# Channel attention with a feed-forward: a fixed order for VectorE's first operations, 24 chunks multiplied early, another layout of the weights

## The chip, the cores and the metric

One Trainium2 chip, of which the program uses one core. The metric is the device time of one execution in microseconds (us), the median of three runs; lower is better.

## The reference

Four batches of q, k and v, each 6080 x 256. The columns of q and k are normalised over the 6080 rows, their 256 x 256 product is put through a softmax, v is multiplied by it, and the result goes through a feed-forward of width 2048 with a leaky ReLU.

```python
qn = q / (np.linalg.norm(q, axis=1, keepdims=True) + 1e-06)
kn = k / (np.linalg.norm(k, axis=1, keepdims=True) + 1e-06)
s = kn.transpose(0, 2, 1) @ qn / tau
a = softmax(s)            # over the last axis, with its maximum taken off
x = (v @ a).reshape(B * S, D)
h = x @ w_in
return np.maximum(0.01 * h, h) @ w_out
```

## The kernel before, in words

Each batch goes through two steps. **Scores:** q and k are read in 48 chunks of up to 128 rows, two chunks to a group and a load. A chunk's product adds to a 256 x 256 sum in PSUM (`Scores.product`), its squares to the column norms (ScalarE squares, VectorE adds). When all chunks are in, the norms, the softmax and its transpose follow (`norms_mm` to `turned_low`). **Feed-forward:** softmax and `w_in` are first multiplied into one matrix per batch (`w_product`, four blocks j, `win` being the split `w_in`), so that a tile of v needs two products only. The first is done in the seven-product scheme of Strassen and Winograd: `w_parts` makes seven weight blocks (A11, A22, A12, S1 to S4) from a block's copy `w_a`, `v_parts` seven operands from a tile of v.

Precision: a float32 value is split into a high part in float32r (a cast) and the rest (a subtraction), and a product is three matmuls in float32r (high-high, high-low, low-high: `PASSES`). A chunk that is multiplied without a split goes through plain float32 matmuls (line 171), one with a split through six float32r ones (line 176).

There are 24 tiles of v of 1024 (or 960) columns with 8 pairs p each, 192 windows in all. A window makes 21 matmuls of the first product (`block_product`, line 546), the activations (`leaky`), and 24 of the second one pair later (`ffn_out`, line 592, on `wo`, the split `w_out`). Side work is queued by window and taken out in slots (`put`, `slot`). The scores of batch b+1 run so beside the feed-forward of batch b.

The start is written out by hand. Batch 0's scores come first. Then the norms and softmax of batch 0, while `fill` multiplies and squares the first 2 x FILL chunks of batch 1 without a split; then `v_parts` of tile 0, `w_product` of block 0 and `w_parts`, then window 0. Blocks 1 to 3 of the weights follow in windows 0 to 6 (`w_early`), and the rest of `w_in` and `w_out`, which come as float64 bits, is converted there (`f64_split`, lines 317 to 333, on tile `f_raw`). Nothing but `tc.issue_after` orders VectorE's operations in the start; a scheduler places the rest. All loads and stores go through one queue, SyncE's.

Of the kernel before, what the change touches and what calls it, by code (L numbers as in the profile page):

```python
# [17 lines left out]
P = 128  # L18
TW = 512
G = 2  # L20
# [3 lines left out]
FILL = 5  # L24
# [7 lines left out]
def channel_attention_ffn(  # L32
# [50 lines left out]
    nc.vector.memset(ones, 1.0)  # L83
    zeros = const.tile([P, P], F32, name="zeros")
    nc.vector.memset(zeros, 0.0)
    exp_bias = const.tile([P, 1], F32, name="exp_bias")
    nc.vector.memset(exp_bias, -896.0 * 2.0**23)
# [16 lines left out]
    class Scores:  # L104


        def __init__(self, b, sizes):
            self.b, self.groups, self.of = b, [], {}
            for n in sizes:
                at = sum(len(x) for x in self.groups)  # L110
                self.of.update({at + x: (len(self.groups), x) for x in range(n)})
                self.groups.append(range(at, at + n))
            self.raw, self.split = {}, {}

        def begin(self, acc, s):
            self.acc, self.s = acc, s
# [45 lines left out]
        def product(self, j):  # L162
            first, last = j == 0, j == NCHUNK - 1
            sp = self.split.pop(j, None)
            raw = self.chunk(j)
            if first:
                nc.tensor.matmul(out=self.s, lhsT=zeros, rhs=raw, start=True, stop=False, skip_group_check=True)
            for h in range(CH):
                hs, s = slice(h * P, (h + 1) * P), self.s[:, h * C:(h + 1) * C]
                if sp is None:  # L170
                    mm = nc.tensor.matmul(  # L171
                        out=s, lhsT=raw[:, 1, hs], rhs=raw[:, 0, :], start=False, stop=last, skip_group_check=True
                    )
                    continue
                for n, (y, z) in enumerate(((0, 0), (0, 1), (1, 0))):
                    mm = nc.tensor.matmul(  # L176
                        out=s, lhsT=sp[:, 1, y, hs], rhs=sp[:, 0, z, :], start=False, stop=last and n == 2,
                        skip_group_check=True,
                    )
            return mm  # L180


        def sums(self):

            acc, other = self.acc
            nc.vector.tensor_tensor(out=acc, in0=acc, in1=other, op=ALU.add)
            nc.vector.tensor_tensor(out=acc[:, :, 0, :], in0=acc[:, :, 0, :], in1=acc[:, :, 1, :], op=ALU.add)
            self.acc = [acc[:, :, 0, :]]
# [190 lines left out]
    A11, A22, A12, S1, S2, S3, S4 = range(NS)  # L379
# [31 lines left out]
    def w_parts(b, j):  # L411
# [71 lines left out]
    wo = const.tile([P, 2, NF, C], F32R, name="w_out_split")  # L483
    FPB = TW // C

    def wo_block(i):
        fs = slice(i * FPB, (i + 1) * FPB)

        def split(raw):
            f64_split(raw, *(wo[:, x, fs, :].rearrange("p f d -> p (f d)") for x in range(2)))  # L490

        return w_out.rearrange("(f p) d -> p f d", p=P)[:, fs, :], split
# [45 lines left out]
    PASSES = ((0, 0), (0, 1), (1, 0))  # L538
# [39 lines left out]
    def ffn_out(i, p):  # L578
# [7 lines left out]
        for name, f, j in (("C11", f1, 0), ("C22", f2, 1), ("C21", f2, 0), ("C12", f1, 1)):  # L586
            sp = g_split.pop((i, p, name))
            early = name in ("C11", "C22")
            for h in range(CH):
                for k, (x, y) in enumerate(((0, 0), (1, 0), (0, 1))):  # L590
                    with in_order("pe"):
                        issued["pe"] = nc.tensor.matmul(  # L592
                            out=o_ps[i][j][h][:, 0:n],
                            lhsT=wo[:, x, f, h * P:(h + 1) * P],
                            rhs=sp[:, y, 0:n],
                            start=p == 0 and early and k == 0,
                            stop=p == NPAIR - 1 and not early and k == 2,
                        )
                    yield
# [47 lines left out]
    def chunk_work(sc, j):  # L647

        put("act", 0.6, lambda: sc.cast(j), [
            ("dve", 0.75, lambda: sc.low(j), [("pe_next", 1, lambda: sc.product(j))]),  # L650
        ])
        if j == 0:
            sc.begin([acc_tile()], bank("s"))
# [90 lines left out]
    for b in range(1, B):  # L744
        w0 = (b - 1) * WPB
        sc = scores[b]
        done = FILL * G if b == 1 else 0
        begin_at, span = (NPAIR, 25) if b == 1 else (2, 31)
        when = {j: w0 + begin_at + (j - done) * span // (NCHUNK - done) for j in range(done, NCHUNK)}
        for i in range(done // G, len(sc.groups)):  # L750
            at(max(w0, when[i * G] - 3), lambda sc=sc, i=i: sc.load(i, qk_raw()))
        for j in range(done, NCHUNK):
            at(when[j], chunk_work, sc, j)
# [9 lines left out]
    sc.begin(  # L763
        [work.tile([P, 2, G, C], F32, name="sq_acc0", tag="qk_split", bufs=3) for _ in range(2)], bank("o", 4)
    )
# [14 lines left out]
    tau_t = const.tile([P, 1], F32, name="tau_t")  # L780
    nc.sync.dma_start(out=tau_t, in_=tau.partition_broadcast(P))
    rtau = const.tile([P, 1], F32, name="rtau")
# [11 lines left out]
    sc.sums()  # L794
    sc.norms_mm()
    sc.norms_taken()
    sc.norms_begun()
    after["dve"] = sc.norms()
    with tc.issue_after(after["load"].ins):
        for i in range(min(2, FILL)):  # L800
            nxt.load(i, qk_raw())
    sc.rows_mm()
    sc.rows_taken()
    after["scaled"] = sc.scaled()
    sc.exps()
    after["normed"] = sc.normed()
    nxt.begin([acc_tile()], bank("s"))
    filled = []

    def fill(n):  # L810
        for i in range(len(filled), min(len(filled) + n, FILL)):
            for j in nxt.groups[i]:
                nxt.product(j)
                if j == 0:
                    nxt.square(j, nxt.acc[0])
                else:
                    sq = temp(name="sq").rearrange("p (x c) -> p x c", x=2)
                    nxt.square(j, sq)
                    nxt.add_square(sq)
            if i + 2 < FILL:  # L820
                nxt.load(i + 2, qk_raw())
            filled.append(i)

    with tc.issue_after(after["dve"].ins):
        fill(2)
    sc.turn("x")
    sc.turned_high()
    after["turned"] = sc.turned_low()
    with tc.issue_after(after["scaled"].ins):
        fill(1)  # L830
        for _, fn in v_parts(0):
            fn()
# [3 lines left out]
    for _, fn in w_parts(0, 0):  # L836
        fn()
    with tc.issue_after(after["turned"].ins):
        fill(FILL)

# [82 lines left out]
```

## Time and profile before

| | |
|---|---|
| median of three runs | 2238.57 us (2238.31 to 2239.28) |
| the profiled execution's own time | 2239.86 us |
| its span | 2238.1 us |
| TensorE (PE) busy | 2189.6 us (98%), 9940 matmuls |
| VectorE (DVE) busy | 1492.8 us (67%) |
| ScalarE (ACT) busy | 1488.8 us (67%) |
| mean granted clock of TensorE | 0.991 |

The chain that ended last is 91% PE. The share of busy time is a mean over stages: the first 210 us or so look different from the rest, and are shown by window below.

### The profile page before, as it was taken

How to read it: one execution, taken by the hardware profiler on the slowest of the kernel's cores; microseconds unless marked ns; L12 is line 12 of the kernel's file. 1: busy time of each engine (PE TensorE's matmuls, PEld its weight loads, DVE VectorE, ACT ScalarE, POOL GpSimd, SP SyncE). 2: the span in 40 equal slices, each digit the busy share in tenths (PEclk: the TensorE clock that was granted, in tenths of full speed). 3: DMA queues.
4: the chain of work that ended last, by engine and by line, in shares of the span. 5: the costliest groups of instructions: out<-in, count | busy, mean ns of one | idle time of the engine just before them, and what ended most of it. 6: DMA issues, size and time to landing. Idle time of an engine off the chain costs nothing.

```text
span 2238.1 us, 27253 instructions
## 1 busy us (share of the span) xinstructions
PE 2189.6 (98%) x9940; PEld 1815.0 (81%) x9940; DVE 1492.8 (67%) x2651; ACT 1488.8 (67%) x2563; POOL 2.8 (0%) x10
## 2 busy tenths in 40 slices
PE   9689999999999999999999999999999999999999
PEld 7467888888888888888887888888888888888887
DVE  7986667666766676666767667677577655555554
ACT  6556777766657777776656777777666666666665
POOL 0000000000000000000000000000000000000000
PEclk9789999999999999999999999999999999999999
DMA  9445343342753434433464344343354432333330
GB/s 347 144 149 191 119 158 138 130 148 84 244 198 111 158 132 137 160 113 139 147 220 164 116 147 156 120 158 129 110 197 149 159 122 85 134 120 104 114 118 35
DMA packets 98966, 324.74 MB, mean 145 GB/s; under 512 B 10256, under 2 KB 22032, under 8 KB 98832
## 3 DMA queue, kind: packets, MB, share of 16 engines
q1 hardware_dynamic: 98832, 323.00, 41.9%
q8 instruction: 78, 1.28, 0.2%
q14 instruction: 56, 0.46, 0.1%
HBM read 264.50 MB, written 58.46 MB: 144 GB/s over the span
## 4 chain that ended last, share of the span: by engine, by line
PE 91%; DVE 5%; ACT 2%; DMA 1%; issue 0%; SPq 0%; DVEq 0%
PE ps_o L592 44%; PE ps_x L546 22%; PE ps_z L546 11%; PE ps_y L546 5%; PE ps_s L176 4%; PE ps_o L171 2%; PE ps_s L395 1%; DVE h L567 1%; DVE g_split L560 1%; ACT h L557 1%; ACT g_split L558 1%; DMA w_dram<-w_rest 1%; DMA f_raw<-in_w_out_dram 0%; DVE w_split L434 0%; DVE v_split L511 0%; DVE f_x L328 0%
## 5 line engine op out<-in xcount | busy, mean ns | idle before, releaser
L592 PE MATMUL ps_o<-g_split,w_out_split 128*128 128x512 f32 (+1 forms) x4608 | 1175.9, 391 | 0.0
L592 PEld LDWEIGHTS ps_o<-g_split,w_out_split 128*128 128x128 f32 x4608 | 868.5, 188 | 180.1
L560 DVE TENSOR_TENSOR g_split<-h,g_split 128x512 fp32r<-128x512 f32 (+1 forms) x768 | 525.4, 684 | 396.1 <-ACT g_split L558 394.6
L546 PE MATMUL ps_x<-v_split,w_split 128*128 128x512 f32 (+1 forms) x2304 | 658.5, 394 | 27.3 <-DVE w_split L433 15.6
L557 ACT ACTIVATE h<-h 128x512 f32<-128x512 f32 (+1 forms) x576 | 362.0, 628 | 290.1 <-DVE h L567 290.1
L573 ACT COPY h<-ps_x 128x512 f32<-128x512 f32 (+1 forms) x576 | 334.3, 580 | 321.8 <-PE ps_x L546 320.4
L546 PEld LDWEIGHTS ps_x<-v_split,w_split 128*128 128x128 f32 x2304 | 423.6, 189 | 118.3 <-ACT h L573 12.0
L558 ACT CAST g_split<-h 128x512 fp32r<-128x512 f32 (+1 forms) x768 | 473.7, 617 | 24.0
L567 DVE TENSOR_TENSOR h<-ps_z,h 128x512 f32<-128x512 f32 (+1 forms) x384 | 262.0, 682 | 293.1 <-ACT h L573 286.5
L546 PE MATMUL ps_z<-v_split,w_split 128*128 128x512 f32 (+1 forms) x1152 | 324.5, 390 | 5.3 <-DVE h L567 5.3
L546 PEld LDWEIGHTS ps_z<-v_split,w_split 128*128 128x128 f32 x1152 | 216.5, 188 | 54.0 <-DVE h L567 7.2
L546 PE MATMUL ps_y<-v_split,w_split 128*128 128x512 f32 (+1 forms) x576 | 163.0, 392 | 0.6 <-ACT w_a L405 0.6
L567 DVE TENSOR_TENSOR h<-ps_y,h 128x512 f32<-128x512 f32 (+1 forms) x192 | 131.3, 684 | 1.9
L546 PEld LDWEIGHTS ps_y<-v_split,w_split 128*128 128x128 f32 x576 | 109.1, 190 | 23.4 <-ACT w_a L405 1.1
L176 PEld LDWEIGHTS ps_s<-qk_split 128*128 128x128 f32 x804 | 114.0, 188 | 12.1 <-issue 1.0
L557 ACT ACTIVATE h<-ps_x 128x512 f32<-128x512 f32 (+1 forms) x192 | 113.1, 589 | 9.6 <-PE ps_x L546 9.6
L176 PE MATMUL ps_s<-qk_split 128*128 128x256 f32 x804 | 117.9, 282 | 0.0
L154 ACT CAST qk_split<-qk_raw 128x512 fp32r<-128x512 f32 x134 | 82.9, 619 | 32.4 <-PE ps_s L176 24.6
L511 DVE TENSOR_TENSOR v_split<-v_raw,v_split 128x512 fp32r<-128x512 f32 (+1 forms) x144 | 98.7, 687 | 4.7
L149 DVE TENSOR_TENSOR sq_acc<-sq_acc,sq 128x512 f32<-128x512 f32 x141 | 96.2, 683 | 0.0
L158 DVE TENSOR_TENSOR qk_split<-qk_raw,qk_split 128x512 fp32r<-128x512 f32 x134 | 91.7, 684 | 2.4 <-ACT qk_split L154 2.4
L146 ACT ACTIVATE sq<-qk_raw 128x512 f32<-128x512 f32 x141 | 88.6, 632 | 1.7 <-DMA qk_raw<-in_k_dram 1.7
(101 smaller groups left out, 728.4 us busy)
## 6 DMA issues: line engine op xcount, KB each, us to landing
w_split<-w_dram SPq DMA_DIRECT2D x184, 896.0 KB, 4.7
qk_raw<-in_q_dram SPq DMA_DIRECT2D x92, 256.0 KB, 3.3
qk_raw<-in_k_dram SPq DMA_DIRECT2D x92, 256.0 KB, 3.7
v_raw<-in_vT_dram SPq DMA_DIRECT2D x40, 512.0 KB, 4.9
out_dram<-o_sb SPq DMA_DIRECT2D x80, 256.0 KB, 4.2
win<-win_dram SPq DMA_DIRECT2D x24, 512.0 KB, 4.2
w_dram<-w_rest SPq DMA_DIRECT2D x24, 512.0 KB, 3.1
w_dram<-w_first SPq DMA_DIRECT2D x24, 384.0 KB, 3.1
```

The source lines that it names most:

```text
L146: return nc.scalar.activation(out=out, in_=self.chunk(j), func=AF.Square)
L149: return nc.vector.tensor_tensor(out=self.acc[0], in0=self.acc[0], in1=sq, op=ALU.add)
L158: return nc.vector.tensor_tensor(out=sp[:, :, 1, :], in0=self.chunk(j), in1=f32(sp[:, :, 0, :]), op=ALU.subtract)
L176: mm = nc.tensor.matmul(out=s, lhsT=sp[:, 1, y, hs], rhs=sp[:, 0, z, :], start=False, stop=last and n == 2, skip_group_check=True,)
L511: last = nc.vector.tensor_tensor(out=sp[:, 1, 0:w], in0=src, in1=f32(sp[:, 0, 0:w]), op=ALU.subtract)
L546: mm = nc.tensor.matmul(out=ps[:, 0:n], lhsT=w[:, x, a, :], rhs=sp[:, y, 0:n], start=first and k == 0, stop=k == 2, skip_group_check=True,)
L557: nc.scalar.activation(out=out[:, 0:n], in_=h[:, 0:n], func=AF.Prelu, alpha=0.01)
L558: issued["act"] = nc.scalar.copy(out=sp[:, 0, 0:n], in_=out[:, 0:n])
L560: issued["dve"] = nc.vector.tensor_tensor(out=sp[:, 1, 0:n], in0=out[:, 0:n], in1=f32(sp[:, 0, 0:n]), op=ALU.subtract)
L567: issued["dve"] = nc.vector.tensor_tensor(out=h[:, 0:n], in0=ps[:, 0:n], in1=h[:, 0:n], op=ALU.add)
L573: issued["act"] = nc.scalar.copy(out=h[:, 0:n], in_=ps[:, 0:n])
L592: issued["pe"] = nc.tensor.matmul(out=o_ps[i][j][h][:, 0:n], lhsT=wo[:, x, f, h * P:(h + 1) * P], rhs=sp[:, y, 0:n], start=p == 0 and earl ...
```

## The change

Four edits. First, `ordered` gives VectorE one order in the start: the norms, the softmax, `v_parts`, `w_parts`, with the softmax first. Second, `FILL` goes from 5 to 12 groups: 24 chunks of batch 1 are multiplied in the start instead of 10, from their own buffers (`qk_fill`, in the ring of `g_split`); they are no longer squared there, but loaded again and squared in windows 8 to 18 (`chunk_work` with `multiply=False`). Third, in batch 0 the casts of `w_parts` and of tile 0's `v_parts` move from VectorE to ScalarE. Fourth, the blocks of `w_split` stand in another order, `PASSES` takes low weights before low operands, and the two halves of `wo` get 128 columns between them.

```diff
-FILL = 5
+FILL = 12
...
+    wo_hl = const.tile([P, 2 * NF * C + P], F32R, name="w_out_split")
+    wo = [wo_hl[:, x:x + NF * C].rearrange("p (f d) -> p f d", d=C) for x in (0, NF * C + P)]
...
-    A11, A22, A12, S1, S2, S3, S4 = range(NS)
+    S1, S2, S3, S4, A22, A12, A11 = range(NS)
...
-                nc.vector.tensor_copy(out=hi, in_=src)
+                (nc.vector.tensor_copy if b else nc.scalar.copy)(out=hi, in_=src)
...
-        nc.vector.tensor_copy(out=sp[:, 0, 0:w], in_=src)
+        (nc.vector.tensor_copy if i else nc.scalar.copy)(out=sp[:, 0, 0:w], in_=src)
...
-    PASSES = ((0, 0), (0, 1), (1, 0))
+    PASSES = ((0, 0), (1, 0), (0, 1))
...
-    def chunk_work(sc, j):
+    def chunk_work(sc, j, multiply=True):
+        if multiply:
+            put("act", 0.6, lambda: sc.cast(j), [
+                ("dve", 0.75, lambda: sc.low(j), [("pe_next", 1, lambda: sc.product(j))]),
+            ])
...
+        quick = 10 if done else 0
+        when = [w0 + begin_at + j * quick // max(done, 1) for j in range(done)]
+        when += [w0 + begin_at + quick + j * (span - quick) // (NCHUNK - done) for j in range(NCHUNK - done)]
...
+            with tc.issue_after(after["load"].ins):
+                nxt.load(i, work.tile([P, 2, G, C], F32, name="qk_fill", tag="g_split", bufs=GBUFS))
             for j in nxt.groups[i]:
                 nxt.product(j)
-                if j == 0:
-                    nxt.square(j, nxt.acc[0])
...
+    ordered(sc.norms_taken, sc.norms_begun, sc.norms)
+    sc.rows_mm()
+    parts = [fn for _, fn in v_parts(0)]
+    ordered(parts[0], sc.rows_taken, sc.scaled)
+    sc.exps()
+    ordered(parts[1], sc.normed)
+    sc.turn("x")
+    sc.turned_high()
+    ordered(parts[2], parts[3], sc.turned_low)
...
+    ordered(*parts[4:8])
+    ordered(*(fn for _, fn in w_parts(0, 0)))
+    ordered(*parts[8:])
+    fill(FILL)
```

On PE, from the end of batch 0's scores to window 0, this stands before (`ps_s` is batch 1's sum, line 194 the norms, 248 the scale's rows, 291 the transpose, 395 the product with `w_in`):

```order
L167 MATMUL ps_s<-qk_raw,zeros 128x512
L171 MATMUL ps_s<-qk_raw 128x256 x8
L194 MATMUL ps_y<-ones,sq_acc_124 128x1 x4
L171 MATMUL ps_s<-qk_raw 128x256 x8
L248 MATMUL ps_y<-diag,ones 128x128 x2
L171 MATMUL ps_s<-qk_raw 128x256 x4
L291 MATMUL ps_x<-ident,s_sb 128x128 x4
L395 MATMUL ps_y<-win_early,aT 128x512 x4
L395 MATMUL ps_z<-win_early,aT 128x512 x4
```

And this with the change, at the same place:

```order
L200 MATMUL ps_y<-ones,sq_acc_126 128x1 x4
L254 MATMUL ps_y<-diag,ones 128x128 x2
L171 MATMUL ps_s<-qk_fill,zeros 128x512
L180 MATMUL ps_s<-qk_fill 128x256 x12
L297 MATMUL ps_x<-ident,s_sb 128x128 x4
L180 MATMUL ps_s<-qk_fill 128x256 x11
L401 MATMUL ps_y<-win_early,aT 128x512 x6
L401 MATMUL ps_z<-win_early,aT 128x512 x6
L180 MATMUL ps_s<-qk_fill 128x256 x25
L551 MATMUL ps_x<-v_split,w_split 128x512 x3
```

The early chunks moved behind the rows of the scale, 12 of their 48 matmuls stand ahead of the transpose, 11 ahead of the product with `w_in`, 25 behind it and ahead of window 0.

On DVE, from the scale (`diag`) to just behind the softmax's maxima (`nm`), this stands before:

```order
L240 TENSOR_SCALAR diag<-ident,rn 128x128 x2
L149 TENSOR_TENSOR sq_acc<-sq_acc,sq 128x512
L255 COPY rq<-ps_y 128x256
L149 TENSOR_TENSOR sq_acc<-sq_acc,sq 128x512
L260 SCALAR_TENSOR_TENSOR s_sb<-ps_o,rk,rq 128x256 x2
L149 TENSOR_TENSOR sq_acc<-sq_acc,sq 128x512
L266 TENSOR_REDUCE nm<-s_sb 128x2
L510 CAST v_split<-v_raw 128x512 x2
```

And this with the change:

```order
L246 TENSOR_SCALAR diag<-ident,rn 128x128 x2
L516 TENSOR_TENSOR v_split<-v_raw,v_split 128x512
L261 COPY rq<-ps_y 128x256
L266 SCALAR_TENSOR_TENSOR s_sb<-ps_o,rk,rq 128x256 x2
L272 TENSOR_REDUCE nm<-s_sb 128x2
L516 TENSOR_TENSOR v_split<-v_raw,v_split 128x512
L285 TENSOR_SCALAR den<-den 128x2
```

The additions of squares left this stretch, and one subtraction for v stands where PE makes the scale's rows, another where ACT takes the exponentials.

On ACT, in window 1, behind the copy of block 1 of the weights (`w_a`; `f_raw`, `f_scale` and `w_out_split` belong to the conversion of `w_out`, `h` and `g_split` to the activations), this stands before:

```order
L405 COPY w_a<-ps_y 128x512
L321 ACTIVATE f_scale<-f_scale,exp_bias 128x512 x2
L557 ACTIVATE h<-h 128x512
L558 CAST g_split<-h 128x512
L332 CAST w_out_split<-f_x 128x512 x2
L323 ACTIVATE f_raw<-f_raw 128x512 x2
L573 COPY h<-ps_x 128x512
```

And this with the change:

```order
L411 COPY w_a<-ps_y 128x512
L439 CAST w_split<-w_a 128x128 x2
L327 ACTIVATE f_scale<-f_scale,exp_bias 128x512 x2
L439 CAST w_split<-w_a 128x256 x2
L562 ACTIVATE h<-h 128x512
L563 CAST g_split<-h 128x512
L439 CAST w_split<-w_s 128x256 x2
L338 CAST w_out_split<-f_x 128x512 x2
L439 CAST w_split<-w_s 128x256 x2
L329 ACTIVATE f_raw<-f_raw 128x512
L578 COPY h<-ps_x 128x512
```

Eight casts came to ACT, four of them on `w_s`, which DVE adds up; they stand ahead of the next copy of `h`.

## Rows read from the trace of the kernel before

**Rows 1.** Windows: us, busy PE, PEld, DVE, ACT, POOL (instructions), PE clock, DMA, GB/s.

```profile
60.00:85.00 25.00, 11.60 (x30) 7.39 (x28) 25.00 (x59) 10.48 (x20) 0.00 (x0) 0.64 0.27 90
85.00:140.00 55.00, 46.26 (x171) 34.43 (x170) 43.94 (x93) 34.80 (x60) 0.00 (x0) 0.88 0.40 150
140.00:210.00 70.00, 57.79 (x235) 44.89 (x234) 54.28 (x115) 42.48 (x74) 0.00 (x0) 0.95 0.50 178
210.00:600.00 390.00, 390.00 (x1827) 325.46 (x1826) 265.34 (x466) 271.34 (x472) 0.00 (x0) 1.00 0.43 146
```

**Rows 2.** PE's longest wait in total, from 85 to 215 us.

```profile
PE ps_x L546 <- DVE w_split L433: 12.1, 3, 5.2
```

**Rows 3.** Timeline of PE, 40 to 62 us: start, us, instruction (two rows a matmul).

```profile
48.70 1.02 PE L167 MATMUL ps_s<-qk_raw,zeros 128*128 128x512 f32 x2
49.55 3.62 PE L171 MATMUL ps_s<-qk_raw 128*128 128x256 f32 x16
53.16 1.05 PE L194 MATMUL ps_y<-ones,sq_acc 128*128 128x1 f32 x8
...
57.80 0.68 PE L248 MATMUL ps_y<-diag,ones 128*128 128x128 f32 x4
59.23 1.99 PE L171 MATMUL ps_s<-qk_raw 128*128 128x256 f32 x8 [0.74 <-DMA qk_raw<-in_k_dram]
```

**Rows 4.** Timeline around the softmax: an addition of squares on DVE, the transpose on PE.

```profile
57.77 0.68 DVE L149 TENSOR_TENSOR sq_acc<-sq_acc,sq 128x512 f32<-128x512 f32 x1
...
66.92 1.17 PE L291 MATMUL ps_x<-ident,s_sb 128*128 128x128 f32 x4 [5.70 <-DVE s_sb L282]
```

**Rows 5.** Timeline of ACT and PE in window 0.

```profile
77.65 1.19 PE L546 MATMUL ps_x<-v_split,w_split 128*128 128x512 f32 x2 [3.53 <-DVE w_split L433]
89.26 0.59 ACT L573 COPY h<-ps_x 128x512 f32<-128x512 f32 x1 [1.97 <-PE ps_x L546]
91.27 0.84 PE L546 MATMUL ps_x<-v_split,w_split 128*128 128x512 f32 x3
```

**Rows 6.** Windows of half a microsecond in which the clock changed its level.

```profile
63.50:64.00 0.50, 0.00 (x0) 0.00 (x0) 0.50 (x2) 0.50 (x2) 0.00 (x0) 0.60 0.00 0
118.00:118.50 0.50, 0.50 (x3) 0.35 (x3) 0.50 (x2) 0.00 (x0) 0.00 (x0) 0.78 0.79 301
```

**Rows 7.** The page's group of split chunks; timeline of PE around one.

```profile
L176 PE MATMUL ps_s<-qk_split 128*128 128x256 f32 x804 | 117.9, 282 | 0.0
...
294.23 0.88 PE L176 MATMUL ps_s<-qk_split 128*128 128x256 f32 x6
294.95 0.88 PE L546 MATMUL ps_x<-v_split,w_split 128*128 128x512 f32 x3
295.66 0.85 PE L546 MATMUL ps_z<-v_split,w_split 128*128 128x512 f32 x3
296.35 1.31 PE L592 MATMUL ps_o<-g_split,w_out_split 128*128 128x512 f32 x5
297.50 0.85 PE L546 MATMUL ps_x<-v_split,w_split 128*128 128x512 f32 x3
```

**Rows 8.** Timeline of DVE and PE before block 1 of the weights is used.

```profile
104.96 0.42 DVE L317 TENSOR_SCALAR f_scale<-f_raw 128x512 int32<-128x512 int32 x1
112.46 0.42 DVE L433 CAST w_split<-w_a 128x128 fp32r<-128x128 f32 x2
112.83 1.71 PE L546 MATMUL ps_x<-v_split,w_split 128*128 128x512 f32 x3 [5.22 <-DVE w_split L433]
114.33 1.48 PE L546 MATMUL ps_y<-v_split,w_split 128*128 128x512 f32 x3
```

**Rows 9.** Timeline of DVE and PE where block 2 of the weights is first used.

```profile
145.47 0.42 DVE L421 TENSOR_TENSOR w_s<-w_a,w_s 128x256 f32<-128x256 f32 x1
146.17 1.19 PE L546 MATMUL ps_x<-v_split,w_split 128*128 128x512 f32 x2 [5.16 <-DVE w_split L433]
148.88 1.48 PE L546 MATMUL ps_y<-v_split,w_split 128*128 128x512 f32 x3
```

More of the change, by code (lines that the diff above doesn't have):

```diff
@@ L167, in product @@
                 nc.tensor.matmul(out=self.s, lhsT=zeros, rhs=raw, start=True, stop=False, skip_group_check=True)
-            for h in range(CH):
-                hs, s = slice(h * P, (h + 1) * P), self.s[:, h * C:(h + 1) * C]
-                if sp is None:
-                    mm = nc.tensor.matmul(
[L172 to L177, printed above, removed]
+            passes = [None] if sp is None else [(0, 0), (0, 1), (1, 0)]
+            for n, of in enumerate(passes):
+                for h in range(CH):
+                    hs, s = slice(h * P, (h + 1) * P), self.s[:, h * C:(h + 1) * C]
+                    if of is None:
+                        lhsT, rhs = raw[:, 1, hs], raw[:, 0, :]
+                    else:
+                        lhsT, rhs = sp[:, 1, of[0], hs], sp[:, 0, of[1], :]
+                    mm = nc.tensor.matmul(
+                        out=s, lhsT=lhsT, rhs=rhs, start=False, stop=last and n == len(passes) - 1,
                         skip_group_check=True,
@@ L645, in acc_tile @@
         return work.tile([P, 2, C], F32, name="sq_acc", bufs=1)
[L647 to L651 removed]
+    def chunk_work(sc, j, multiply=True):
[3 more added lines that the diff above has]
+            ])
         if j == 0:
[L653 removed]
+            sc.acc = [acc_tile()]
             put("act", 0.6, lambda: sc.square(0, sc.acc[0]))
@@ L748, in channel_attention_ffn @@
         begin_at, span = (NPAIR, 25) if b == 1 else (2, 31)
-        when = {j: w0 + begin_at + (j - done) * span // (NCHUNK - done) for j in range(done, NCHUNK)}
-        for i in range(done // G, len(sc.groups)):
+        quick = 10 if done else 0
+        when = [w0 + begin_at + j * quick // max(done, 1) for j in range(done)]
+        when += [w0 + begin_at + quick + j * (span - quick) // (NCHUNK - done) for j in range(NCHUNK - done)]
+        if b > 1:
+            at(when[0], lambda sc=sc: setattr(sc, "s", bank("s")))
+        for i in range(len(sc.groups)):
             at(max(w0, when[i * G] - 3), lambda sc=sc, i=i: sc.load(i, qk_raw()))
-        for j in range(done, NCHUNK):
-            at(when[j], chunk_work, sc, j)
+        for j in range(NCHUNK):
+            at(when[j], chunk_work, sc, j, j >= done)
         e = w0 + begin_at + span + 1
@@ L762, in channel_attention_ffn @@
     sc, nxt = scores[0], scores[1]
-    sc.begin(
-        [work.tile([P, 2, G, C], F32, name="sq_acc0", tag="qk_split", bufs=3) for _ in range(2)], bank("o", 4)
-    )
+    sc.acc = [work.tile([P, 2, G, C], F32, name="sq_acc0", tag="qk_split", bufs=3) for _ in range(2)]
+    sc.s, nxt.s = bank("o", 4), bank("s")
     n0 = len(sc.groups)
@@ L793, in channel_attention_ffn @@
             conv.split()
[L794 to L807, printed above, removed]
     filled = []
@@ L811, in fill, with ordered @@
         for i in range(len(filled), min(len(filled) + n, FILL)):
+            with tc.issue_after(after["load"].ins):
+                nxt.load(i, work.tile([P, 2, G, C], F32, name="qk_fill", tag="g_split", bufs=GBUFS))
             for j in nxt.groups[i]:
                 nxt.product(j)
-                if j == 0:
-                    nxt.square(j, nxt.acc[0])
[L816 to L821, printed above, removed]
-            filled.append(i)
-    with tc.issue_after(after["dve"].ins):
-        fill(2)
+            filled.append(i)
+    def ordered(*fns):
+        for fn in fns:
+            with in_order("dve"):
+                issued["dve"] = fn()
+    sc.sums()
+    issued["dve"] = sc.last_sum
+    sc.norms_mm()
+    ordered(sc.norms_taken, sc.norms_begun, sc.norms)
[4 more added lines that the diff above has]
+    ordered(parts[1], sc.normed)
     sc.turn("x")
     sc.turned_high()
[L828 to L832, printed above, removed]
+    ordered(parts[2], parts[3], sc.turned_low)
     for h in range(CH):
```

25 lines of the change are left out of this document (10 added, 15 removed).

## The prediction

> **What bounds the kernel now.** I read the windows first. From 210 to 600 us PE is busy 390.00 of 390.00 us at clock 1.00, while DVE has 265 and ACT 271 [rows 1]: there the time is PE's work, and only fewer or shorter matmuls change it. From 60 to 85 us it is the other way round: DVE is busy 25.00 of 25.00 and PE 11.60. From 85 to 210 PE lacks 55 - 46.26 + 70 - 57.79 = 20.9 us, and its clock is down at times [rows 1]. So I read next what PE waited for there: 12.1 us in three waits for DVE's casts of the weights, line 433 [rows 2]. The change therefore acts on two accounts: PE's work in the long stage, which is worth its full length, and the start, where it matters when DVE's chain lets PE go.
>
> **The moved products.** The page counts 804 matmuls of split chunks, six a chunk, so 134 of 192 - 48 = 144 chunks; ten of batch 1 went early. With 24 early, 14 x 6 = 84 float32r matmuls leave the long stage. One chunk there takes from 294.23 to 294.95, 0.72 us [rows 7], and PE has no gap to give it back: **-10.1 us**. This term is the firmest: nothing moves into PE's place. What ACT and DVE do instead (24 squares and additions for early chunks, no casts or lows for them) is about what they did before, 0.6 to 0.7 us an operation, in 30% and more of free time [rows 1]. Batch 1's first 12 groups are read twice now, 36 group loads for 24: some 6 MB more, on DMA engines that are 43% busy [rows 1], issued three windows ahead; I cost them at nothing. Without that lead a late group would cost its own landing, a few us.
>
> **The fill.** Sixteen rows, four plain chunks, took 3.62 us at full clock, 0.90 a chunk, and the opening matmul with zeros 0.85 [rows 3]. So the early work grows to 24 x 0.90 + 0.85 = 22.5 us, all of it ahead of window 0 in PE's order. It costs what it sticks out behind DVE's chain, so I lay out PE's time anew:
> - Batch 0's product ends at about 48.7 and the norms' matmuls still start at 53.16, the scale's rows at 57.80 [rows 3], since the chain of sums and Newton steps ahead of them is the same.
> - SyncE's queue puts seven transfers of 0.5 MB ahead of the first early group that stood behind it (two loads of `w_out`, two of `w_in`, three stores of `win`). The fifth early group, the 39th such transfer, landed at 59.2, and PE waited 0.74 us for it [rows 3]: some 1.4 us each, as an estimate. The first early group is now the 38th, so it lands at about 57.8, and the next ones come faster than PE's 1.8 a group. So the fill starts at about 58.4, behind the rows, and loads do not hold it. One load of `w_out` stands ahead of batch 0's last three groups: 1.4 us at most, which DVE's queue of additions covers. Behind the last early group stand only stores of block 0 and the load of tile 1, due windows later.
> - PE is then idle from 48.7 to 53.2 and from 54.2 to 57.8. In the trace the clock fell at 63.7 [rows 6], 2.5 us after PE's last matmul ended (59.23 + 1.99 = 61.2 [rows 3]). So I take it that the fill begins at the lower level, half the rate (1.2 for 2.4 GHz). From 112.83, where PE worked without a break, the clock came back at 118.2, after 5.4 us [rows 6, 8]. Half of that is lost: 2.6 us.
> - The transpose waits for 12 of the 48 fill matmuls now: 58.4 + 0.85 + 6 x 0.90 + 2.6 = 67.2. It started at 66.92 before, waiting for the softmax [rows 4]. That one gets faster by four additions of 0.6 us ahead of its maxima and sums [rows 4] and ends around 63; so the new order on DVE alone frees nothing, the fill takes its place.
> - Transpose (0.7) and the product with `w_in` (12 x 0.23, the step in [rows 7]) are added: window 0 starts at 58.4 + 22.5 + 2.6 + 0.7 + 2.8 = **87.0**, where its first matmul stood at 77.65 [rows 5]. By then `w_parts` is done: its input is there at about 76.5, and DVE needs some 7 us behind that.
> - Before, window 0 was torn by waits and at half clock; its sixth product began at 91.27 [rows 5]. Now: two products 1.4, drain 0.2, then DVE 0.69, ACT three times 0.6, a product 0.7, six matmuls 1.4 and hops 0.2 = 6.4 us, so 93.4. The start is **+2.1 us** later.
>
> At this place a rule speaks for another sum. By the Trainium skill, Perfetto Trace Analysis, section Engine Utilization, a float32 high-low matmul has half the normal rate. The rows disagree: 0.45 us against 0.12 for 256 columns, 3.8 times. By the page's figure the fill would be about 11 us, DVE's chain would set window 0 at about 83, and the time would be 2223 to 2224.
>
> **The blocks of weights in windows 2 and 4.** The high casts go to ACT. For block 1, DVE is busy without a gap from 104.96 to the cast at 112.46, and PE's matmul follows at 112.83 [rows 8]; the same additions and conversions stand ahead of the first subtraction now, 0.2 us long instead of the cast's. So PE's second matmul, which needs that low part, comes at about 112.8: only the first one is won, and the second product starts at 113.6 instead of 114.33 [rows 8], -0.7. For block 2 one conversion step (0.6) moved behind the subtraction, and the low half no longer comes 2 us after the high one: second product at 146.5 instead of 148.88 [rows 9], -2.4. Block 3 I leave at nothing. Sum **-3.1 us**. Both ends: nothing, if ACT's copies of `h`, which queue behind casts that wait for DVE's `w_s`, lose what is won (8 casts a block, 3 us on ACT); -8, if the waits of 12.1 us [rows 2] shrink by two thirds.
>
> **The layout.** No row shows a matmul with other distances. Two differ in the trace: three matmuls on `w_split`, whose halves lie 3,584 bytes apart, take 295.66 to 296.35, 0.230 each; five on `wo`, halves 16,384 bytes apart, 296.35 to 297.50, 0.230 each [rows 7]. Equal to a nanosecond, so I take nothing. One nanosecond over 8,640 matmuls would be 8.6 us; I keep that as both ends.
>
> **The sum.** -10.1 + 2.1 - 3.1 = -11.1. The profiled execution took 2239.86 us, 1.3 above the median of the runs, so 2228.8 on its own terms and 2238.57 - 11.1 = **2227.5** on the median's.
>
> **Rivals.**
> - *The fill stays at half clock* (slower). If the clock does not come back until PE's float32 matmuls are through, 22.5 us become 45 and with the transpose and the product behind it some 48: 20 to 23 more, 2248 to 2250. It decides from 28 us of half rate on, where the gain is used up (11.1 + 2.6 = half of 28). For it: no row shows the clock rising under float32 matmuls. Against it: it stood at 1.00 under the same instructions until 61 us. 6%.
> - *The clock is not lost, or DVE's relief reaches further*: 2.6 less in the fill, or the waits shrink to a third: 2220 to 2224. PE's idle stretches of 4.5 and 3.6 us speak against the first, DVE's unbroken queue against the second. 18%.
> - *ACT takes DVE's place.* Casts on `w_s` wait in ACT's queue for DVE, and the copy of `h` that frees PE's bank stands behind them. At 2 to 3 us a block for three blocks, the gain in windows 2 to 6 turns round: 2232 to 2236. ACT is busy 42 to 63% there [rows 1], which speaks against a bound, not against single waits. 15%.
> - *The layout counts.* 1 ns less or more for each matmul: 2219 or 2236. Equal steps on two layouts speak against it. 6% and 7%.
> - *No difference*: the moved products are lost again in the start (fill at 10 us more than counted, by late loads behind SyncE's stores and clock): 2235 to 2242. 6%.
>
> **How the numbers follow.** The forecast (2225 to 2231) has 42%. The rest goes as above. 0.2%, 4.5 us, is about what a measurement of this kernel can tell from none: faster is below 2234.1. That holds for the forecast, the second case, most of ACT's and the fast layout (0.42 + 0.18 + 0.10 + 0.06), and for a few of the others: 0.79. Within 0.2%: 0.12. Slower: 0.09. The range, 2219 to 2237, leaves out the slow clock and the tail of no difference above, and the sum of two gains below.
>
> **What would show it.** Right: 720 matmuls on the split line instead of 804, with the step of 0.72 us; a fill that starts at 58 to 59, runs 5 us at half rate and ends at about 87 with PE busy throughout; no wait of PE between 58 and 87; DVE's waits for block 2 down by 2 us; a matmul step of 0.230 as before. Wrong: PE waiting for `qk_fill` loads; a clock of 0.5 beyond 66 us; copies of `h` waiting on casts; another step of line 592's matmuls, which would outweigh everything else.

## The result, and the profile after

The changed kernel takes **2211.95 us** (2211.19 to 2212.84), the kernel before in the same session 2238.61: ratio 0.9878, interval 0.9863 to 0.9894, or 26.7 us less. The forecast was 2227.5, the range 2219 to 2237; the time lies below both.

I read after in the order of the forecast. First the start. Windows of after that answer to [rows 1], and four windows of 1 us each (columns as there):

```profile
60.00:85.00 25.00, 25.00 (x110) 21.36 (x109) 18.48 (x41) 10.35 (x24) 0.00 (x0) 0.93 0.72 241
85.00:140.00 55.00, 45.47 (x181) 34.34 (x180) 40.72 (x78) 37.29 (x69) 0.00 (x0) 0.94 0.37 134
140.00:210.00 70.00, 57.63 (x228) 44.91 (x227) 49.66 (x96) 44.60 (x87) 0.52 (x1) 0.93 0.52 182
210.00:600.00 390.00, 390.00 (x1801) 326.38 (x1800) 270.97 (x479) 276.43 (x484) 0.52 (x1) 1.00 0.46 158
...
53.00:54.00 1.00, 0.96 (x7) 0.87 (x6) 0.00 (x1) 0.25 (x1) 0.00 (x0) 0.62 1.02 378
58.00:59.00 1.00, 1.00 (x5) 0.87 (x5) 0.42 (x2) 0.00 (x0) 0.00 (x0) 0.50 1.01 406
63.00:64.00 1.00, 1.00 (x5) 0.84 (x4) 0.97 (x3) 0.00 (x0) 0.00 (x0) 0.76 0.00 0
64.00:65.00 1.00, 1.00 (x6) 0.89 (x5) 0.34 (x1) 0.00 (x0) 0.00 (x0) 1.00 0.13 20
```

From 60 to 85 PE is now the engine without a gap, and DVE has 6.5 us free. The clock falls to its lower level (0.50) in the microsecond from 53, after PE had stood idle for 3.8 us, and is back at its upper level during the microsecond from 63 to 64. Timeline of PE in after (a plain float32 matmul has two rows, as in [rows 3]):

```profile
57.55 1.19 PE L254 MATMUL ps_y<-diag,ones 128*128 128x128 f32 x4 [3.59 <-DVE diag L246]
58.53 1.92 PE L171 MATMUL ps_s<-qk_fill,zeros 128*128 128x512 f32 x2
60.24 6.95 PE L180 MATMUL ps_s<-qk_fill 128*128 128x256 f32 x24
67.03 0.60 PE L297 MATMUL ps_x<-ident,s_sb 128*128 128x128 f32 x4
...
74.98 10.95 PE L180 MATMUL ps_s<-qk_fill 128*128 128x256 f32 x50
85.59 1.05 PE L551 MATMUL ps_x<-v_split,w_split 128*128 128x512 f32 x3
...
92.17 0.84 PE L551 MATMUL ps_x<-v_split,w_split 128*128 128x512 f32 x3
...
115.20 1.48 PE L551 MATMUL ps_y<-v_split,w_split 128*128 128x512 f32 x3
...
146.87 1.48 PE L551 MATMUL ps_y<-v_split,w_split 128*128 128x512 f32 x3
...
157.34 1.65 PE L551 MATMUL ps_x<-v_split,w_split 128*128 128x512 f32 x3 [5.04 <-ACT h L578]
```

The fill begins at 58.53 (58.4 forecast), the transpose at 67.03 (67.2), window 0 at 85.59 (87.0), its sixth product at 92.17 (93.4). Block 1's second product comes at 115.20, later than in [rows 8]. Block 2's comes at 146.87, 2.0 us sooner than in [rows 9]; but ten microseconds later PE waits 5 us for a copy of `h`. PE's waits of after, 85 to 215 us, answer to [rows 2]:

```profile
PE ps_x L551 <- ACT h L578: 10.5, 7, 5.0
PE ps_x L551 <- DVE w_split L440: 10.2, 3, 4.7
```

Timeline of ACT ahead of that copy:

```profile
150.49 0.68 ACT L329 ACTIVATE f_raw<-f_raw 128x512 f32<-128x512 uint32 x1 [1.56 <-DMA f_raw<-in_w_out_dram]
154.46 0.65 ACT L329 ACTIVATE f_raw<-f_raw 128x512 f32<-128x512 uint32 x1 [3.29 <-DMA f_raw<-in_w_out_dram]
...
156.71 0.58 ACT L578 COPY h<-ps_x 128x512 f32<-128x512 f32 x1
```

The copy stands in ACT's queue behind a conversion that waits for its load. In before the same conversion ran at 152.09:

```profile
152.09 0.69 ACT L323 ACTIVATE f_raw<-f_raw 128x512 f32<-128x512 uint32 x1 [1.06 <-DMA f_raw<-in_w_out_dram]
```

To see where the 27 us came from, I cut both traces at the first matmul of window 8, of window 48 (tile 6) and of the last window. The windows view, first product's line alone (us; busy PE and PEld with counts; clock, DMA, GB/s); 21 x 8 = 168 matmuls stand ahead of window 8, 840 between it and window 48. Before, and then after:

```profile
0.00:201.37 201.37, 52.47 (x168) 33.83 (x169) 0.91 0.58 209
201.37:650.42 449.05, 216.96 (x840) 154.68 (x840) 1.00 0.44 150
650.42:2218.49 1568.07, 777.97 (x3004) 556.46 (x3004) 1.00 0.40 137
```

```profile
0.00:202.98 202.98, 49.28 (x169) 32.15 (x169) 0.93 0.63 224
202.98:638.63 435.65, 215.75 (x841) 155.66 (x840) 1.00 0.47 161
638.63:2191.11 1552.48, 773.21 (x3004) 556.04 (x3003) 1.00 0.41 138
```

In these two traces the start costs 1.6 us, the stretch in which batch 1 is multiplied gives 13.4, and the rest, where the change adds no operation and takes none away, gives 15.6. That last figure is what I had not counted. The page's groups of matmuls show it (busy, mean ns of one). Before:

```profile
L592 PE MATMUL ps_o<-g_split,w_out_split 128*128 128x512 f32 (+1 forms) x4608 | 1175.9, 391 | 0.0
L546 PE MATMUL ps_x<-v_split,w_split 128*128 128x512 f32 (+1 forms) x2304 | 658.5, 394 | 27.3 <-DVE w_split L433 15.6
L546 PE MATMUL ps_z<-v_split,w_split 128*128 128x512 f32 (+1 forms) x1152 | 324.5, 390 | 5.3 <-DVE h L567 5.3
```

After:

```profile
L597 PE MATMUL ps_o<-g_split,w_out_split 128*128 128x512 f32 (+1 forms) x4608 | 1164.5, 388 | 0.0
L551 PE MATMUL ps_x<-v_split,w_split 128*128 128x512 f32 (+1 forms) x2304 | 651.0, 390 | 21.3 <-ACT h L578 10.5
L551 PE MATMUL ps_z<-v_split,w_split 128*128 128x512 f32 (+1 forms) x1152 | 322.8, 388 | 3.4 <-DVE h L572 3.4
L180 PE MATMUL ps_s<-qk_split 128*128 128x256 f32 x720 | 105.9, 283 | 0.0
```

The second product's 4,608 matmuls are the same in number, order and operands, and take 11.4 us less, 2.5 ns each; the first product's largest group (`ps_x`) takes 7.5 us less. My reasons for 0 were wrong there, and most of the experiments are about it.

The kernels differ in two orders that the four edits of the description do not name. `exp_bias`, `tau_t` and `rtau` now stand ahead of `w_out_split` and the zeros behind it. And the six float32r matmuls of a split chunk go pass by pass, where they went half by half; every run below on the changed kernel keeps that. No gain shows on their line: 117.9 us over 804 before and 105.9 over 720 after, 147 ns each in both.

### The profile page after: what moved, and what is told of

The parts are those of the page before. It is cut to its first block, busy times and chain, and to the rows that moved or that the text cites. A ratio compares the mean times of both kernels' runs of the same rounds, so it can differ in the third digit from the quotient of the medians.

```text
span 2210.1 us, 27204 instructions
## 1 busy us (share of the span) xinstructions
PE 2169.7 (98%) x9912; PEld 1811.7 (82%) x9912; DVE 1472.3 (67%) x2598; ACT 1487.3 (67%) x2588; POOL 3.3 (0%) x11
## 4 chain that ended last, share of the span: by engine, by line
PE 90%; DVE 5%; DMA 3%; ACT 2%; issue 0%; SPq 0%; DVEq 0%; ACTq 0%
PE ps_o L597 44%; PE ps_x L551 22%; PE ps_z L551 11%; PE ps_y L551 6%; PE ps_s L180 4%; PE ps_s L401 2%; DVE h L572 1%; DMA qk_raw<-in_q_dram 1%; DVE g_split L565 1%; ACT g_split L563 1%; DMA qk_raw<-in_k_dram 1%; ACT h L562 1%; DMA w_dram<-w_rest 1%; DMA f_raw<-in_w_out_dram 0%; DVE f_x L334 0%
## 5 line engine op out<-in xcount | busy, mean ns | idle before, releaser
L597 PE MATMUL ps_o<-g_split,w_out_split 128*128 128x512 f32 (+1 forms) x4608 | 1164.5, 388 | 0.0
L551 PE MATMUL ps_x<-v_split,w_split 128*128 128x512 f32 (+1 forms) x2304 | 651.0, 390 | 21.3 <-ACT h L578 10.5
L180 PEld LDWEIGHTS ps_s<-qk_split 128*128 128x128 f32 x720 | 102.2, 190 | 10.2 <-issue 1.0
L180 PE MATMUL ps_s<-qk_split 128*128 128x256 f32 x720 | 105.9, 283 | 0.0
L158 ACT CAST qk_split<-qk_raw 128x512 fp32r<-128x512 f32 x120 | 74.2, 619 | 31.4 <-PE ps_s L180 27.5
L162 DVE TENSOR_TENSOR qk_split<-qk_raw,qk_split 128x512 fp32r<-128x512 f32 x120 | 82.1, 684 | 2.3 <-ACT qk_split L158 2.3
```

Of the source, the lines that this page charges most:

```text
L162: return nc.vector.tensor_tensor(out=sp[:, :, 1, :], in0=self.chunk(j), in1=f32(sp[:, :, 0, :]), op=ALU.subtract)
L180: mm = nc.tensor.matmul(out=s, lhsT=lhsT, rhs=rhs, start=False, stop=last and n == len(passes) - 1, skip_group_check=True,)
L551: mm = nc.tensor.matmul(out=ps[:, 0:n], lhsT=w[:, x, a, :], rhs=sp[:, y, 0:n], start=first and k == 0, stop=k == 2, skip_group_check=True,)
L597: issued["pe"] = nc.tensor.matmul(out=o_ps[i][j][h][:, 0:n], lhsT=wo[x][:, f, h * P:(h + 1) * P], rhs=sp[:, y, 0:n], start=p == 0 and earl ...
```

## The experiments

Each stands beside runs of the kernel before on the same chip (medians 2238.9 to 2239.7). "Second product" below is the busy time of the 4,608 matmuls on `w_out_split`, 1164.5 us in after.

### The three edits that look like the layout, one by one

```diff
-    PASSES = ((0, 0), (1, 0), (0, 1))            # e1
+    PASSES = ((0, 0), (0, 1), (1, 0))
-    ... for x in (0, NF * C + P)]                # e2
+    ... for x in (0, NF * C)]
-    S1, S2, S3, S4, A22, A12, A11 = range(NS)    # e3
+    A11, A22, A12, S1, S2, S3, S4 = range(NS)
```

> The changed kernel with PASSES of the first product put back to high-high, high-low, low-high; nothing else. Theory (each of the three layout edits sets the step of the line it touches, so the 11.4 us that line 597 gave belong to the gap in w_out_split and the 7.5 us of line 551 to the blocks' order and the order of passes): line 597 stays at 1164.5 us, line 551 goes up from 651.0 by 3 to 7 us, the time by as much, to 2215 to 2219. Rival 1 (the gap of 128 columns alone, or addresses that moved with it, made all matmuls faster): nothing changes, 2212. Rival 2 (the order of passes made it all): both lines go back, 2230.

> The changed kernel with the low half of w_out_split right behind the high half again (16,384 bytes apart for 16,896); the tile keeps its size, so every other address stays. Theory (the distance between the halves sets line 597's step): line 597 goes from 1164.5 back to about 1175.9 us, line 551 stays at 651.0, the time is 2223 to 2224. Rival 1 (other addresses that moved, such as those of the operands, made the step): nothing changes, 2212. Rival 2 (order of passes or blocks): nothing changes, 2212.

> The changed kernel with the weight blocks in the order A11, A22, A12, S1 to S4 again; nothing else. Theory: line 551 goes up from 651.0 by 2 to 5 us, line 597 stays at 1164.5; the time is 2214 to 2217. Rival (the order of passes alone made line 551's gain): 2212, line 551 at 651.

2210.86, 2211.95 and 2211.38: none of the three moved anything, and the second product took 1164.6, 1165.4 and 1164.7 us. My theory that each sets its own line's step fell.

### All of the layout undone

e4 takes back the three edits above together, and puts `w_out_split`, the zeros and the small constants where they stood.

> The changed kernel with all of the layout undone: w_out_split in one piece where it stood before, the small constants in their old order, old order of blocks, old order of passes. The order on VectorE, the 24 early chunks and the casts on ScalarE stay. Theory (the excess over my forecast is the matmul step, and the step is the layout): line 597 back at about 1176 us, line 551 at about 658, the time 2228 to 2231, which is where the rest of my sum stood. Rival (the step got shorter by something else, as fewer operations beside it, or the start gave the excess): 2212 to 2216.

**2227.12**, ratio to before 0.9946 (0.9933 to 0.996): 12.0 us below before, where my sum, which has nothing for the layout, had 11.1; the time lies just below the theory's 2228 to 2231 and far from the rival's. The three stretches of this kernel:

```profile
0.00:200.91 200.91, 49.25 (x169) 31.94 (x169) 0.95 0.63 227
200.91:640.08 439.17, 216.92 (x841) 155.63 (x841) 1.00 0.47 159
640.08:2204.79 1564.71, 777.44 (x3003) 555.85 (x3003) 1.00 0.40 137
```

Window 8 to 48 takes 439.17, 9.9 less than before: the moved products, forecast 10.1. The last stretch is within 3.4 us of before's, and the two executions lie 2.6 apart by themselves (1.3 below the median here, 1.3 above it there). From e4 to after, the middle stretch gives 3.5 us and the last one 12.2: together 15.7, what the layout is worth.

### Which part of it

e5 is e1, e2 and e3 at once, with the sizes of the tiles kept. In e6 the zeros and then `exp_bias` stand ahead of `w_out_split` again, `tau_t` and `rtau` behind it. In e7 the tile is shorter:

```diff
+    zeros = const.tile([P, P], F32, name="zeros")                       # e6
+    exp_bias = const.tile([P, 1], F32, name="exp_bias")
     wo_hl = const.tile([P, 2 * NF * C + P], F32R, name="w_out_split")
...
-    wo_hl = const.tile([P, 2 * NF * C + P], F32R, name="w_out_split")   # e7
+    wo_hl = const.tile([P, 2 * NF * C], F32R, name="w_out_split")
```

> The changed kernel with the order of passes, the order of the blocks and the distance of the halves of w_out_split all undone at once; tile sizes and so all addresses stay as in the changed kernel. Each alone moved nothing. Theory now (the step comes from where the tiles lie in SBUF, not from the three edits): 2211 to 2213, the matmuls of the second product at 1164 to 1166 us. Rival (any one of the three suffices, and only without all of them the step is long): 2227, the matmuls of the second product at 1176 us.

> The changed kernel with the small constants and the zeros in front of w_out_split again, so that w_out_split starts 448 bytes further on, at the place of before; all tiles behind it (operands, temporaries, w_split) stay where the changed kernel has them. Theory A (the place of the operand rings and temporaries sets the step): 2211 to 2213, second product at 1164 to 1166 us. Theory B (the place of w_out_split does): 2222 to 2228, second product at 1176 us, the first product as now. Theory C (the zeros in front or behind): as B in time, but all matmuls longer.

> The changed kernel with w_out_split 128 columns shorter and without the gap, so that every tile behind it lies 512 bytes lower, at the place of before; w_out_split itself, the constants and the orders stay as in the changed kernel. Theory A (place of operand rings and temporaries): 2226 to 2228, second product at 1176 us, ScalarE and VectorE busy some 4 us more, as where all of the layout was undone. Theory B (place of w_out_split): 2211 to 2213.

2211.78, **2227.7** and 2212.6. So the three edits together do nothing, nor do 512 bytes for all the tiles behind; the 15.8 us come with the order of the constants, that is with `w_out_split` starting 448 bytes further on. Theory B had the time and the second product right, but not "the first product as now": its `ps_x` group takes 5.5 us more than in after, though nothing that it reads has moved. Theory C, the place of the zeros, had longer matmuls everywhere; the pads below bear on it. Groups of e6:

```profile
L597 PE MATMUL ps_o<-g_split,w_out_split 128*128 128x512 f32 (+1 forms) x4608 | 1175.5, 391 | 0.0
L551 PE MATMUL ps_x<-v_split,w_split 128*128 128x512 f32 (+1 forms) x2304 | 656.5, 393 | 19.4 <-DVE w_split L440 10.0
```

### The same alone in the kernel before, and other distances

e9 is the kernel before with the constants in the order of the change and nothing else. e10 to e12 are the changed kernel with n = 32, 64 and 128 bytes ahead of the tile:

```diff
-    zeros = const.tile([P, P], F32, name="zeros")                       # e9
+    exp_bias = const.tile([P, 1], F32, name="exp_bias")
+    tau_t = const.tile([P, 1], F32, name="tau_t")
+    rtau = const.tile([P, 1], F32, name="rtau")
+    wo = const.tile([P, 2, NF, C], F32R, name="w_out_split")
+    zeros = const.tile([P, P], F32, name="zeros")
...
+    const.tile([P, n // 4], F32, name="pad")                            # e10, e11, e12
-    wo_hl = const.tile([P, 2 * NF * C + P], F32R, name="w_out_split")
+    wo_hl = const.tile([P, 2 * NF * C + P - n // 4], F32R, name="w_out_split")
```

> The kernel before with one thing changed: exp_bias, tau_t and rtau stand ahead of w_out_split and the zeros behind it, so that w_out_split starts 448 bytes lower, as in the changed kernel; operand rings and all orders stay. Theory (the place of w_out_split makes the whole of the step's gain): the second product's matmuls at 1164 to 1166 us, the time 15 to 16 us below before, 2223 to 2225. Rival (the place acts only together with the changed order of work): 2230 to 2239.

> The changed kernel with a pad of 32 bytes ahead of w_out_split and its halves together; the tile is shortened by as much, so that nothing behind it moves, and the zeros stay behind it. w_out_split then starts at a multiple of 256 bytes. Theory i (w_out_split must stand at the same remainder of 512 bytes as w_split and the operands, 224): 2222 to 2228. Theory ii (the remainder of 128 bytes matters, 96 being good and 32 bad): no forecast for 0; as good as now if even starts are good, 2211 to 2213. Theory iii (not the place of w_out_split but that of zeros and constants): 2211 to 2213.

> As the run with 32 bytes, with a pad of 64: remainder 288 of 512, 32 of 128 bytes. Theory i: 2222 to 2228. Theory ii: 2222 to 2228. Theory iii: 2211 to 2213.

> As the run with 32 bytes, with a pad of 128: remainder 352 of 512, 96 of 128 bytes. Theory i: 2222 to 2228. Theory ii: 2211 to 2213. Theory iii: 2211 to 2213.

e9: **2224.03**, 14.9 below before (0.9931, 0.9918 to 0.9945), as expected, with the second product at 1163.4 us: this edit alone is worth more than all the rest of the change (12.0 us by e4). The pads were a surprise: **2239.97, 2243.2, 2244.37**. Theories ii and iii fall; theory i has the sign, with twice the size. 32 bytes cost 28 us. The zeros stand behind `w_out_split` in all three, so its place is enough by itself, without theory C of e6. Group of e10:

```profile
L598 PE MATMUL ps_o<-g_split,w_out_split 128*128 128x512 f32 (+1 forms) x4608 | 1187.9, 393 | 0.0
```

### What the place must agree with

```diff
+    const.tile([P, 8], F32, name="pad")                   # e13: ahead of ident, so ahead of all
+    const.tile([P, 128], F32, name="pad")                 # e14: ahead of w_out_split alone
+    work.tile([P, 8], F32, name="pad_w", bufs=1)          # e15: ahead of w_split
```

In e14 the tile is shortened by as much as its pad takes. The pad of e15 moves the tiles behind `w_split` too (outputs, accumulators, the small tiles of norms and softmax). e16 has the pads of e10 and e15. e17 has that of e10, one of 8 columns ahead of the ring `g_split` and one of 120 columns behind it.

> The changed kernel with a pad of 32 bytes ahead of every tile, so that constants, w_out_split, operands, temporaries and w_split all start 32 bytes further on and stand to one another as in the changed kernel. Theory R (tiles must stand at the same remainder of 512 bytes to one another): 2211 to 2213. Theory P (the place itself matters, a remainder of 224 being good and 256 bad): 2240 or more, since w_out_split stands where it stood with the pad of 32 bytes.

> The changed kernel with w_out_split alone 512 bytes further on (its halves together), all else in place. Theories R and P with a period of 512 bytes: 2211 to 2213. Rival (a longer period, or the exact place): 2227 to 2244.

> The changed kernel with w_split (and the output and accumulator tiles behind it) 32 bytes further on, w_out_split and the operand rings in place. Theory R1 (the two sorts of weights to each other): as with 32 bytes for w_out_split, 2235 to 2245, the longer steps where weights of one sort follow those of the other. Theory R2 (weights to the moving operands of the same matmul): the first product's 4,032 matmuls slower by 4 to 5 ns, 2228 to 2232, the second product at 1164 us. Theory P: 2225 to 2235. No effect: 2212.

> The changed kernel with w_out_split and w_split both 32 bytes further on, the operand rings in place. Theory R1 (the two sorts of weights to each other): 2211 to 2213. Theory R2 (weights to moving operands): 2250 to 2270, all 8,640 matmuls slower. Theory P: 2240 to 2270.

> The changed kernel with w_out_split 32 bytes further on, and with it the ring g_split alone, whose tiles are the moving operands of the second product; a pad of 480 bytes behind that ring puts everything behind it at 512 bytes, so at the same remainder as before, and v_split, temporaries and w_split stand to one another as in the changed kernel. Theory R2 (weights and moving operand of the same matmul): 2210 to 2214, second product at 1164 to 1166 us. Rival (w_out_split against w_split, or against the temporaries that ScalarE and VectorE use): 2235 to 2245, second product at 1185 us or more. Both at once: between.

**2209.82** with everything 32 bytes on, **2211.82** with `w_out_split` alone 512 on: what counts is the place of the tiles to one another and no fixed place, and 512 bytes make no difference (128 cost 32 us; 256 were not tried). By that period e6's 448 bytes on are 64 short. **2236.76** for `w_split` without `w_out_split`, which lies in R1's range and not in R2's; **2256.97** for both sorts of weights: moved together the two sorts of weights agree with each other and still cost 45 us, where each alone costs 25 and 28. So they must agree with something that stayed; R1 falls. I took that to be the moving operand, R2, and **2235.97** for e17 refutes this as the whole of it: with `g_split` moved along, the second product gets back only a part. The time lies in the range of the rival, the second product below the rival's 1185. Its group in e13, e15, e16 and e17:

```profile
L598 PE MATMUL ps_o<-g_split,w_out_split 128*128 128x512 f32 (+1 forms) x4608 | 1164.6, 388 | 0.0
```

```profile
L599 PE MATMUL ps_o<-g_split,w_out_split 128*128 128x512 f32 (+1 forms) x4608 | 1175.5, 390 | 0.0
L553 PE MATMUL ps_z<-v_split,w_split 128*128 128x512 f32 (+1 forms) x1152 | 328.1, 393 | 3.5 <-DVE h L574 3.5
```

```profile
L600 PE MATMUL ps_o<-g_split,w_out_split 128*128 128x512 f32 (+1 forms) x4608 | 1191.4, 394 | 0.0
```

```profile
L598 PE MATMUL ps_o<-g_split,w_out_split 128*128 128x512 f32 (+1 forms) x4608 | 1179.2, 391 | 0.0
L552 PE MATMUL ps_z<-v_split,w_split 128*128 128x512 f32 (+1 forms) x1152 | 327.5, 392 | 3.6 <-DVE h L573 3.6
```

The row to look at is e15's first. Of what the two products read only `w_split`, the weights of the *first* one, was moved, and the *second* product's matmuls take 11 us more. e17's second row says the same the other way round: the first product's operands stand right, and it is slower by 4.7 us in this group. A misplaced tile slows matmuls that don't read it.

The traces say more on two questions. Take a step to be the time from the start of a matmul on `w_out_split` to the start of the next matmul, between 210 and 2190 us, without steps over 400 ns, which are waits.

- *Do other engines' accesses make it?* The mean step is 225.3 ns in after, 227.8 in e15, 228.7 in e17 and 231.3 in e16. The 52 to 63 steps a trace during which ACT, DVE and POOL were idle and no DMA packet was under way take 224.8, 230.6, 231.6 and 233.0 ns (each to within 1.5). The delay is there in full without them.
- *Which matmuls are slowed?* In e15, the steps of matmuls with another sort of matmul just ahead or behind grow from 225.4 to 230.4 ns, those between two of their own sort from 225.2 to 226.5. In the traces PE loads a matmul's weights while the one ahead of it runs (in after, a load and a matmul both begin at 1010.89 us, the load's own matmul at 1011.1), so neighbours could well be the partners. But in e17 both sorts of steps are long (228.4 and 228.8), and that does not fit.

### The other terms

```diff
-FILL = 12                              # e8
+FILL = 8
-        quick = 10 if done else 0
+        quick = 5 if done else 0
...
-                (nc.vector.tensor_copy if b else nc.scalar.copy)(out=hi, in_=src)   # e18, and so
+                nc.vector.tensor_copy(out=hi, in_=src)                              # in v_split_of
```

> The changed kernel with 8 early groups for 12 (and the second load's squares in 5 windows for 10). 8 chunks go back to the long stage: 48 float32r matmuls, 8 x 0.72 = +5.8 us there. PE has 8 x 0.9 = 7.2 us less to do ahead of window 0. Theory of my prediction (the fill sets when window 0 begins): window 0 begins 4 to 7 us earlier, but its sixth product waits for VectorE's and ScalarE's operands, so that half at most is kept: 2212 to 2217. Rival 1 (the fill is free, other work sets the end of the start): 2217 to 2219. Rival 2 (the fill costs its full length): 2210 to 2212.

> The changed kernel with batch 0's casts of w_parts and v_parts back on VectorE. My sum's third term (the casts on ScalarE give 0.7 us in block 1 and 2.4 in block 2): 2214 to 2216. Rival 1 (the trace of the changed kernel has block 1's second product at 115.20, no sooner than before, so the casts gave nothing): 2211 to 2213. Rival 2 (the casts on VectorE also lengthen its chain ahead of window 0 and there the fill hides them, but block 1 waits for all of its eight): 2217 to 2220.

e8: **2216.5**, 4.5 more than after, as my theory had it. Window 0 begins at 78.75, 6.8 us sooner, and its sixth product at 89.24, 2.9 sooner. At window 8 (201.50) 1.5 is left, which says little: traces with the start and the layout of after reach window 8 between 199.97 (e13) and 203.74 (e5). The stretch to window 48 takes 441.92, 6.3 more (5.8 forecast). e18: **2212.14**, no change: rival 1. Its waits of PE from 85 to 215:

```profile
PE ps_x L551 <- DVE w_split L439: 12.3, 3, 5.3
PE ps_x L551 <- ACT h L578: 6.2, 6, 1.6
PE ps_x L551 <- DVE w_split L440: 1.4, 1, 1.4
```

With the casts on VectorE PE waits 13.7 us for weights and 6.2 for copies; with them on ScalarE 10.2 and 10.5. The sum is 19.9 and 20.7.

## Why the prediction was wrong

| term | forecast | measured | from |
|---|---|---|---|
| moved products | -10.1 | -9.9 | e4, window 8 to 48 |
| fill, to window 0's sixth product | +2.1 | +0.9 (e13: -1.0) | timeline, 92.17 to 91.27 |
| casts, blocks 1 and 2 | -3.1 | about 0 | e18; block 2 won 2.0, then lost |
| start in all, to window 8 | -1.0 | +1.6 (e13: -1.4, e4: -0.5, e5: +2.4) | windows |
| layout | 0 | -15.8 | e6 to after; -14.9 by e9 |

**The step that failed** is "Equal to a nanosecond, so I take nothing", the term for the layout, and the ends of 8.6 us with it. The layout gave 15.8 us, 1.8 ns on each of 8,640 matmuls. Without it the kernel takes 2227.12 (e4) where I had 2227.5.

The rows were read rightly and did not bear on the question: I took matmuls on `w_split` and on `w_out_split` in one program for two layouts. e6 shows that `w_out_split` in the place of before lengthens the matmuls on `w_split` as well (`ps_x` from 651.0 to 656.5 us), so both rows of before were already long. The bound was too narrow by its own group too: in [rows 7] the three matmuls from 294.95 to 295.66 are 0.237 apart and the next ones 0.230. Seven nanoseconds over 8,640 matmuls are 60 us. I also named the wrong edits: distance of the halves, block order and passes, which move nothing (e1, e2, e3, e5). The line that did it, four constants written in another order, I read as a tidying and gave no term. My rival "The layout counts" had the sign, at 2219 and 6%; and the last of my signs of being wrong, another step of the second product's matmuls that outweighs everything else, is what came.

That 2227.5 and 2227.12 agree so well is partly luck. The fill cost less than its term, the casts gave nothing for their 3.1, and e4's last stretch is 3.4 us shorter than before's, for which I had no term.

**The moved products** were right, mechanism and size: 720 matmuls on the split line, PE without a gap from 210 to 600.

**The fill** was right in its mechanism. Fill and transpose came within 0.2 us of the forecast, and the lower level ended about 5.0 us after the fill's start (5.4 forecast; half of that is 2.7, where my sum has 2.6). Window 0 came 1.4 sooner. At the upper level 25 matmuls (two rows each) take from 74.98 to 85.59, 0.42 us each; I had 0.45. The sixth product came at 92.17 in after, but between 90.27 (e13) and 92.02 (e7) in other traces with this start and layout, so +0.9 is one sample. By the rule of the Trainium skill (Perfetto Trace Analysis, section Engine Utilization) that a high-low float32 matmul runs at half the normal rate, my estimate had window 0 at about 83. The trace does not agree: 0.42 us stands against 0.12 for a float32r matmul of 256 columns [rows 7], and window 0 began at 85.59.

**The blocks** fell. Block 2's second product came 2.0 us sooner (2.4 forecast), block 1's not at all: 115.20, 0.9 later than before, which is the delay of the start. What block 2 won went at 157.34: the copy of `h` that frees PE's bank stood behind a conversion that waited 3.29 us for its load, and window 5 began at 166.46, before at 163.20. My rival "ACT takes DVE's place" had this queue and this copy, but casts on `w_s` in front, and 15%; the wait was for a DMA. The same order of work reached window 8 at 202.98 in after, at 199.97 in e13 and at 203.74 in e5, so I can't tell a start of -1.0 from one of nothing. The load came late for two reasons that the trace shows: SyncE issued it at 148.9 (147.5 before), when VectorE's line 330 had read its buffer for the last time, and the four loads took up to 5.5 us to land (4.6 before). That the casts on ScalarE made line 330 late is argued: in e18, without them, the same conversion waited 1.24 us.

**Still open** is what the tiles must agree with. Shown is: with the weights, the operand rings and the temporaries at one remainder of 512 bytes the kernel is fast wherever they stand (after, e13, e14); weights 32 bytes off against everything else cost 25 to 28 us; matmuls are slowed that don't touch the misplaced tile (e6, e15); agreement with the own moving operand alone does not suffice (e17). By the Trainium skill (SBUF — State Buffer, section SBUF: two separate sides) PE never waits for another engine's access, which would leave only PE's own operands. The traces agree: the steps are as long while the other engines are idle. Which of PE's reads gets in the way of which was not separated, and neighbours alone do not explain e17.

## What to carry to other kernels

Where one engine's stream is the bound, give a term to every edit that moves a tile in memory, an innocent reordering of constants too: a nanosecond a matmul is 8.6 us here, and 32 bytes cost 28 us. A pad of a few bytes ahead of the weights is a cheap experiment, and worth it before any rescheduling: in the kernel before, the order of four constants alone gave 14.9 us (e9), more than all the rescheduling. And two rows from one program are no test of a property that acts on the whole program.

## What was unexpected in the hardware

Matmuls of float32r, 512 columns, with the same operands and order, took per matmul (second product's busy time over 4,608) 253 ns in the fast place, 255 with `w_out_split` 64 bytes short of it (e6), 258 with it 32 bytes past it and 259 with both sorts of weights 32 past. 512 bytes made no difference, nor did 32 for all tiles together. The delay is as long while no other engine and no DMA is at work. The mechanism is not known from these runs.
